# Preparing K and Q of an attention unit two units ahead, and starting a gated block one step earlier

## The chip, the cores and the metric

One core of a Trainium2 chip runs the whole program. The metric is the device time of one execution in microseconds (us), and less is better. The times given are medians of repeated executions; the profile is one execution more, with a time of its own.

## The reference

Attention over 4 batches, 8 heads, 576 positions, head size 64, with a threshold: scores lower than the row's maximum by more than tau are dropped. Then a gated feed-forward block on 2304 tokens of width 512, then a second one with a leaky ReLU:

```
scores = scale * q @ k^T                       # (4, 8, 576, 576)
keep   = scores >= max(scores) - tau
attn   = softmax(where(keep, scores, -1e9)) @ v
x      = attn as (2304, 512)
x      = (((x @ w1) * (x @ w2)) @ w3) @ w_out  # d_ff 1024
h      = x @ w_in                              # d_ff 2048
out    = maximum(0.01 * h, h) @ w_out2
```

All of it is fp32. The kernel multiplies `w3` by `w_out` once, so that the gated block is two products and one product more.

## The kernel before

The tokens are cut into six column groups of 384 (`gid` 0 to 5). Attention is cut into 32 units: a unit is a pair of heads `p` and a piece of one batch's queries that lies in one column group. A unit is made of steps, 80 in all. Units 0 to 3 (group 0), 12 to 19 (groups 2 and 3) and 28 to 31 (group 5) have three steps of 128 queries for each of the two heads. Units 4 to 11 (group 1) and 20 to 27 (group 4) have two steps, and are called tailed: the first (`c is None`) takes 64 queries of both heads as one block of 128 rows, the second takes 128 queries of each head. For the first, the two heads' Q blocks are put on the diagonal of a zeroed 128 x 128 tile, `qz`, or, where the operands are split, `qzs`. There is one of each.

Units 0 to 7 multiply fp32 operands in one pass. From unit 8 on (`PER = 8`) K and Q are split into a high part `qkh` and a low part `qkl` (fp32r), and a score takes three passes (`PASSES`). Before either, Q is multiplied by the scale `scl` on VectorE.

A step `n` of the main loop does this, in the order in which the code writes it:

- `load_halves` decodes a part of the weights (in the first steps), and `mask(n)` applies the threshold and normalises `e`: VectorE, with one multiplication on ScalarE (L298).
- `scale_unit(u + 1)` in the last step of a unit below 7: VectorE scales Q and writes `qz` (L213, L218).
- `scores(n + 1)`: TensorE (L267), row maximum on VectorE (L274), exponential on ScalarE (L275).
- `split_unit(u + 1)` in the first step of a unit: scale on VectorE (L231), `qkh` on ScalarE (L234), `qkl` on VectorE (L235), and for a tailed unit four copies into `qzs` on VectorE (L241).
- `weighted(u - 1)`, the product with V (L354), in the first step of a unit; its result goes to `xr` (L358).
- `transposes(n)`: a two-head step transposes `e` of head 0 into the PSUM tile `tp`, which ScalarE copies to `HH` (L338), then `e` of head 1 into the same tile, which VectorE copies (L334), then `tq`. There is one `tp`: the second four transposes wait for the first copy.
- Around the transposes stand pieces of six matmuls of a gated block (`gated`, `psab` L435 and `psh` L455). These are the filler. A two-head step has four of them, a tail step two.
- `load_v(u + 1)` and `load_unit(u + 2)` in the first step of a unit.

When the last unit of a column group is done, its gated block is put in a queue as due two steps later: `queue.append((n + 2, gid))`. At that step `split_x` splits the group's `xr` tiles (cast on ScalarE L366, difference on VectorE L367), and the block's pieces become the filler of the steps after. In the first steps there is no gated block; the product of `w3` and `w_out` (L405) and dummy matmuls stand between the transposes.

What sets the order: TensorE runs in the order of the code, by hand, from end to end. The queue of SP, which issues the loads, runs in the order of the code until the block of group 1 is due. VectorE, ScalarE and GpSimd are ordered during attention by a scheduler that simulates the program; a few instructions, the scaling among them, are kept in program order. From the second feed-forward block on all engines are ordered by hand.

Of the kernel before, what the change touches and what calls it, by code (L numbers as in the profile page):

```python
# [13 lines left out]
ALU = mybir.AluOpType  # L14
# [4 lines left out]
B, H, S, D = 4, 8, 576, 64  # L19
# [8 lines left out]
KS = D + S  # L28
# [7 lines left out]
UNITS = tuple(  # L36
    (b + i, p, g) for b in range(0, B, 2)
    for several in (((0, 0),), ((0, 1), (1, 0)), ((1, 1),)) for p in range(4) for i, g in several)
STEPS = tuple((u, c) for u, (b, p, g) in enumerate(UNITS) for c in PARTS[b % 2][g][2])
NS = len(STEPS)  # L40
PER = 8
# [7 lines left out]
def attention_gated_ffn(ctx: ExitStack, tc: tile.TileContext, qkv, tau, w3t, wout, w12, w2, out):  # L49
# [6 lines left out]
    nc = tc.nc  # L56

    def f(ap):
        return ap.bitcast(F32)
# [17 lines left out]
    qz = apool.tile([P, P], F32, name="qz")  # L77
# [4 lines left out]
    qzs = apool.tile([P, 2, P], F32R, name="qzs")  # L82
# [3 lines left out]
    scl = cpool.tile([P, 1], F32, name="scl")  # L86
# [77 lines left out]
    qk_t, vv_t = {}, {}  # L164

    def piece_of(u):

        b, p, g = UNITS[u]
        gq, gw, blocks = PARTS[b % 2][g]
        at = b * S + gq  # L170
        return gq, gw, blocks[0] is None, at // GW, at % GW
# [29 lines left out]
            nc.sync.dma_start(out=vv[:, a, :NK - 1], in_=src[:, :NK - 1])  # L201
            nc.sync.dma_start(out=vv[r, a, NK - 1], in_=src[r, NK - 1])

    def scale_unit(u):

        if u >= PER:
            return
        _, gw, tailed, _, _ = piece_of(u)
        qk = qk_t[u]
        if tailed:  # L210
            for a in range(2):
                o = a * D
                tc.keep_in_program_order(nc.vector.tensor_scalar(  # L213
                    out=qz[o:o + D, o:o + D], in0=qk[o:o + D, KS:KS + D], scalar1=scl[o:o + D],
                    scalar2=None, op0=ALU.mult))
        q = qk[:, KS + (D if tailed else 0):KS + gw]
        tc.keep_in_program_order(
            nc.vector.tensor_scalar(out=q, in0=q, scalar1=scl, scalar2=None, op0=ALU.mult))  # L218

    qks_t = {}  # L220

    def split_unit(u):

        if not PER <= u < len(UNITS):
            return
        _, gw, tailed, _, _ = piece_of(u)
        n = KS + gw
        qk = qk_t[u]
        q = qk[:, KS:n]
        tc.keep_in_program_order(  # L230
            nc.vector.tensor_scalar(out=q, in0=q, scalar1=scl, scalar2=None, op0=ALU.mult))  # L231
        hi = wld.tile([P, 1024], F32R, tag="st", name="qkh", bufs=4)
        lo = wld.tile([P, 1024], F32R, tag="st", name="qkl", bufs=4)
        nc.scalar.copy(hi[:, :n], qk[:, :n])  # L234
        nc.vector.tensor_tensor(out=lo[:, :n], in0=qk[:, :n], in1=f(hi[:, :n]), op=ALU.subtract)  # L235
        qks_t[u] = (hi, lo)
        if tailed:
            for i, part in enumerate((hi, lo)):
                for a in range(2):
                    r = slice(a * D, a * D + D)  # L240
                    nc.vector.tensor_copy(qzs[r, i, r], part[r, KS:KS + D])  # L241


    sc_t, e_t = {}, {}

# [36 lines left out]
    def mask(n):  # L282
        u, c = STEPS[n]
        sc, ths, st = sc_t.pop(n)
        for a, th in enumerate(ths):
            ev = e_t[n][:, a * S:a * S + S].rearrange("p (a b) -> p a b", a=2)
            nc.vector.scalar_tensor_tensor(  # L287
                out=ev, in0=sc[a][:, :, :HS], scalar=th, in1=ev, op0=ALU.is_ge, op1=ALU.mult,
                accum_out=st[:, a:a + 1])
        m = len(ths)  # L290
        nc.vector.tensor_scalar(out=st[:, :m], in0=st[:, :m], scalar1=1e-9, scalar2=None, op0=ALU.add)
        nc.vector.reciprocal(st[:, :m], st[:, :m])  # L292
        for a in range(m):
            ev = e_t[n][:, a * S:a * S + S]
            if a == m - 1:
                nc.vector.tensor_scalar(out=ev, in0=ev, scalar1=st[:, a:a + 1], scalar2=None, op0=ALU.mult)
            else:
                nc.scalar.activation(ev, ev, AF.Copy, scale=st[:, a:a + 1])  # L298
        if c is None:
            nc.gpsimd.tensor_copy(e_t[n][:, S:S + D], e_t[n][:, S - D:S])  # L300
# [42 lines left out]
    def weighted(u):  # L343

        _, gw, _, gid, at = piece_of(u)
        p = UNITS[u][1]
        vv = vv_t[u]
        HH, tail = he_t.pop(u), tl
        av = ps_w.tile([P, 512], F32, tag="w", name="av")
        for i in range(NK):  # L350
            for a in (1, 0):
                kc = (4, 0, 1, 2, 3)[i]
                rhs = (HH[:, kc, a] if kc < 4 else tail)[:, :gw]
                nc.tensor.matmul(  # L354
                    av[a * D:a * D + D, :gw], vv[:, a, kc], rhs, start=(i == 0), stop=(i == NK - 1))
        if (gid, p) not in x_t:
            x_t[gid, p] = xpool.tile([P, GW], F32, tag="xr", name="xr")
        nc.scalar.copy(x_t[gid, p][:, at:at + gw], av[:, :gw])  # L358
# [120 lines left out]
    load_v(0)  # L479
    load_unit(1)  # L480
    issue()
    scale_unit(0)
    halves_in = [0]
    folded = [0]

    def load_halves(k):
        for _ in range(k):
            if next(loads, 0) != 0:
                halves_in[0] += 1
# [9 lines left out]
    def fold_some(most, halves):  # L499

        while most and folded[0] < 2 * KF and piece(folded[0]) <= halves:
            next(folding, 0)
            folded[0] += 1
            most -= 1

    def keep_busy(k):

        scratch = ps_w.tile([P, 512], F32, tag="w", name="scratch")
        for _ in range(k):
            nc.tensor.matmul(scratch[:, :P], ident, ident, start=True, stop=True)  # L510
# [7 lines left out]
    queue = []  # L518
# [3 lines left out]
    def more(k):  # L522

        for _ in range(k):
            open_[0] = next(filler, False)

    for n in range(NS):
        u, c = STEPS[n]
        gid = piece_of(u)[3]
        weight = 1 if c is None else 2  # L530
        first_of_unit = n == 0 or STEPS[n - 1][0] != u
        last_of_unit = n == NS - 1 or STEPS[n + 1][0] != u
        decoded = halves_in[0]
        kh = 2 if n == 0 else 3
        load_halves(kh // 2)
        mask(n)
        if last_of_unit:
            scale_unit(u + 1)
        if n + 1 < NS:
            scores(n + 1)  # L540
        if n and first_of_unit:
            split_unit(u + 1)
        due += rate * weight

        if weigh:
            while open_[0]:
                more(1)
                due -= 1
            weighted(weigh.pop())
        k = max(0, int(due))  # L550
        due -= k
        parts = [(k + 2) // 3, (k + 1) // 3, k // 3]

        def fill(i):
            more(parts[i])
            if i < 2:
                fold_some(1, decoded)

        fill(0)
        pieces = transposes(n)  # L560
        next(pieces)
        fill(1)
        for _ in pieces:
            pass
        if last_of_unit:
            weigh.append(u)
        fill(2)
        if n < 3:
            keep_busy(7)
        if first_of_unit:  # L570
            load_v(u + 1)
            load_unit(u + 2)
        load_halves(kh - kh // 2)
        if last_of_unit and (n == NS - 1 or piece_of(u + 1)[3] != gid):
            queue.append((n + 2, gid))
        if queue and queue[0][0] == n:
            _, gid = queue.pop(0)
            while halves_in[0] < 32:
                load_halves(1)
            fold_some(2 * KF, 32)  # L580
            next(folding, 0)
            for _ in filler:
                pass
            if gid == 0:
                s_ld.close()
                gpool = s_ffn.enter_context(tc.tile_pool(name="gpool", bufs=8, reuse_waits="tile"))
                fpool = s_ffn.enter_context(tc.tile_pool(name="fpool", bufs=2, reuse_waits="tile"))
            if gid == 1:
                while halves_in[0] < 40:
                    load_halves(1)  # L590
                in_order.close()
            filler = gated(gid, split_x(gid))
            rate, due, open_[0] = 2.04, 0.0, False
# [38 lines left out]
    def issue():  # L632
        while len(raws) < min(used[0] + 3, len(order)):
            j, c = order[len(raws)]
            st = wld.tile([P, 1024], I32, tag="st", name="st", bufs=4)
            nc.sync.dma_start(out=st, in_=w2[j, :, c * 512:c * 512 + 512].bitcast(I32))
            raws.append(st)
# [305 lines left out]
    for n in range(total):  # L943
        ci, q = divmod(n, NQ)
# [71 lines left out]
```

## Time and profile before

| | before |
|---|---|
| median of 3 executions | 1050.05 us (1049.09 to 1051.96) |
| profiled execution | 1044.59 us |
| its span in the profile | 1042.8 us |
| TensorE matmul busy | 1006.2 us (96%) |
| VectorE / ScalarE / GpSimd busy | 644.2 / 574.5 / 235.3 us |
| granted TensorE clock, mean | 0.992 |
| TensorE idle in the span | 36.6 us |

The span starts with the first instruction on record and ends with the last. The 1.8 us by which the profiled execution's time exceeds it lie outside. Attention takes about the first 600 us of the span; the second feed-forward block has the rest.

### The profile page before, as it was taken

The page shows a single profiled execution, that of the slowest core. Times are in us where ns is not written, and L with a number is a line of the kernel's source. Part 1 is how long each engine was busy: PE and PEld are TensorE (multiplying, and loading weights), DVE is VectorE, ACT ScalarE, POOL GpSimd, SP SyncE. Part 2 cuts the span into 40 slices and gives each one's busy share as a digit, 9 for nine tenths or more (in the row PEclk, how much of TensorE's full clock was granted, in tenths as well). Part 3 has the DMA queues.
Part 4 walks back from the last instruction along what each step waited for, and adds up shares of the span by engine and source line. Part 5 has one row for each costly group of instructions (what it writes and reads, how often), then busy time and mean ns, then how long its engine had stood idle before and what let it go on. Part 6 is the DMA issues. An engine that isn't in the chain of part 4 may idle for free. (4 is left out here: it accounts for less than half of the span.)

```text
span 1042.8 us, 16142 instructions
## 1 busy us (share of the span) xinstructions
PE 1006.2 (96%) x5896; PEld 851.5 (82%) x5896; DVE 644.2 (62%) x1367; ACT 574.5 (55%) x1068; POOL 235.3 (23%) x219
## 2 busy tenths in 40 slices
PE   7899979999999999999999999999999999999998
PEld 5444458888888888888888899999988999999997
DVE  7889787788786777688877646275774111621111
ACT  5677674556565555455556536487874333543332
POOL 2335451100110110011001135245452111411110
PEclk9999989999999999999999999999999999999999
DMA  9644332223211111222211025578644953055401
GB/s 289 216 163 143 118 106 56 56 80 100 53 32 52 36 29 48 69 60 70 75 32 53 28 84 184 207 272 325 198 157 159 417 195 127 1 221 208 187 1 60
DMA packets 52126, 129.50 MB, mean 124 GB/s; under 512 B 15696, under 2 KB 30032, under 8 KB 48208
## 3 DMA queue, kind: packets, MB, share of 16 engines
q1 hardware_dynamic: 51904, 128.48, 35.9%
q8 instruction: 46, 0.75, 0.3%
q14 instruction: 32, 0.26, 0.1%
q10 hardware_dynamic: 144, 0.00, 0.0%
HBM read 95.95 MB, written 32.51 MB: 123 GB/s over the span
## 5 line engine op out<-in xcount | busy, mean ns | idle before, releaser
L435 PE MATMUL psab<-x,w 128*128 128x384 f32 x1152 | 233.6, 346 | 0.0
L925 PE MATMUL po<-dn,gg 128*128 128x512 f32 x864 | 222.9, 390 | 0.0
L435 PEld LDWEIGHTS psab<-x,w 128*128 128x128 f32 x1152 | 195.7, 188 | 11.4 <-DVE e L287 5.4
L925 PEld LDWEIGHTS po<-dn,gg 128*128 128x128 f32 x864 | 160.0, 188 | 22.0
L890 PE MATMUL ps<-h,uph 128*128 128x384 f32 x672 | 172.8, 338 | 1.1 <-DVE sum L872 0.6
L872 DVE TENSOR_TENSOR sum<-snap,ps 128x384 f32<-128x384 f32 x72 | 39.8, 552 | 173.9 <-PE ps L890 162.4
L275 ACT ACTIVATE e<-sc,nm 128x576 f32<-128x576 f32 x144 | 100.9, 738 | 70.8 <-DVE nm L274 70.7
L890 PEld LDWEIGHTS ps<-h,uph 128*128 128x128 f32 x672 | 123.5, 188 | 15.1 <-DVE sum L872 1.3
L448 POOL TENSOR_TENSOR gt<-at,gt 128x384 fp32r<-128x384 f32 x48 | 50.2, 1045 | 376.3 <-ACT gt L447 376.3
L274 DVE TENSOR_REDUCE nm<-sc 128x1 f32<-128x576 f32 x144 | 103.6, 752 | 40.8 <-PE sc L267 40.0
L287 DVE SCALAR_TENSOR_TENSOR e<-sc,nm,e 128x576 f32<-128x576 f32 x144 | 113.1, 815 | 13.5 <-ACT e L275 8.7
L455 PE MATMUL psh<-gt,w 128*128 128x384 f32 x576 | 114.1, 344 | 0.0
L890 PE MATMUL ps<-h,upl 128*128 128x384 f32 x336 | 113.1, 337 | 0.0
L880 POOL TENSOR_TENSOR gg<-sum,gg 128x384 fp32r<-128x384 f32 x48 | 50.4, 1050 | 254.3 <-ACT gg L879 230.5
L455 PEld LDWEIGHTS psh<-gt,w 128*128 128x128 f32 x576 | 98.1, 188 | 4.8 <-issue 2.4
L332 PE MATMUL tp<-ident,e 128*128 128x128 f32 x512 | 78.5, 276 | 10.9 <-ACT HH L338 10.7
L332 PEld LDWEIGHTS tp<-ident,e 128*128 128x128 f32 x512 | 63.5, 141 | 26.9 <-ACT HH L338 13.0
L867 ACT COPY snap<-ps 128x384 f32<-128x384 f32 x72 | 34.3, 477 | 88.7 <-PE ps L890 88.7
L298 ACT ACTIVATE e<-e,nm 128x576 f32<-128x576 f32 x64 | 49.7, 777 | 40.8 <-DVE nm L292 40.3
L334 DVE COPY HH<-tp 128x512 f32<-128x512 f32 x64 | 44.2, 690 | 39.5 <-PE tp L332 39.4
L354 PE MATMUL av<-HH,vv 128*64 128x384 f32 (+1 forms) x512 | 67.6, 406 | 0.0
L877 ACT ACTIVATE sum<-sum 128x384 f32<-128x384 f32 x72 | 37.8, 525 | 48.1 <-DVE sum L872 48.1
(117 smaller groups left out, 1428.6 us busy)
## 6 DMA issues: line engine op xcount, KB each, us to landing
st<-in_w SPq DMA_DIRECT2D x48, 512.0 KB, 5.6
dn<-dn_d SPq DMA_DIRECT2D x10, 1024.0 KB, 7.4
uph<-up_d SPq DMA_DIRECT2D x10, 896.0 KB, 8.4
upl<-up_d SPq DMA_DIRECT2D x10, 896.0 KB, 4.6
vv<-in_qkv SPq DMA_DIRECT2D x64, 128.0 KB, 2.2
raw<-in_w3t SPq DMA_DIRECT2D x8, 1024.0 KB, 6.7
dn_d<-dn SPq DMA_DIRECT2D x8, 1024.0 KB, 6.7
up_d<-uph SPq DMA_DIRECT2D x8, 896.0 KB, 4.6
```

What stands on the lines that cost most here:

```text
L274: nc.vector.tensor_reduce(out=nm, in_=sc[a][:, :, :HS], op=ALU.max, axis=AX.XY, negate=True)
L275: nc.scalar.activation(e[:, a * S:a * S + S].rearrange("p (a b) -> p a b", a=2), sc[a][:, :, :HS], AF.Exp, bias=nm)
L287: nc.vector.scalar_tensor_tensor(out=ev, in0=sc[a][:, :, :HS], scalar=th, in1=ev, op0=ALU.is_ge, op1=ALU.mult, accum_out=st[:, a:a + 1])
L298: nc.scalar.activation(ev, ev, AF.Copy, scale=st[:, a:a + 1])
L332: nc.tensor.transpose(tp[:, kc], e[:, k0:k0 + P], ident)
L354: nc.tensor.matmul(av[a * D:a * D + D, :gw], vv[:, a, kc], rhs, start=(i == 0), stop=(i == NK - 1))
L435: nc.tensor.matmul(ps, w12_t[i][:, a, mat * 512 + kk * P:mat * 512 + kk * P + P], xt[kk][:, c], start=(m == 0), stop=(m == 11))
L448: nc.gpsimd.tensor_tensor(out=gt[i][:, 1], in0=at, in1=f(gt[i][:, 0]), op=ALU.subtract)
L455: nc.tensor.matmul(ps, w34_t[i // 2][:, a, i % 2, o * P:o * P + P], gt[i][:, c], start=(m == 0), stop=(m == 23))
L880: eng.tensor_tensor(out=gg[:, 1], in0=gf, in1=f(gg[:, 0]), op=ALU.subtract)
L890: nc.tensor.matmul(ps, (uph, upl)[a][:, wi, i * P:i * P + P], hs[k][:, c, i], start=(opens[k] and m == 0), stop=(m == 5), skip_group_check ...
L925: nc.tensor.matmul(po_t[o], gg[:, c, t * P:t * P + P], dn[:, i, a], start=(q == 0 and seen[o] == 1 and m == 0), stop=(q == NQ - 1 and seen ...
```

## The change

The code that scales Q and the code that splits K and Q become one function, `prepare_unit`, which runs for unit `u + 2` in the last step of unit `u`, behind `scores(n + 1)` (before: the scaling for `u + 1` in the last step of `u`, ahead of `scores(n + 1)`; the splitting for `u + 1` in the first step of `u`). For the first eight units it scales the whole piece, the tail block too. The copies that place the tail block, `place_tail(u + 1)`, run in the first step of unit `u`, behind `mask(n)` and ahead of `scores(n + 1)`, one step before the tail's scores. A gated block is due one step behind its last unit's last step, not two.

```diff
-    def scale_unit(u):
-        if u >= PER:
-            return
...
-        if tailed:
-            for a in range(2):
-                o = a * D
-                tc.keep_in_program_order(nc.vector.tensor_scalar(
-                    out=qz[o:o + D, o:o + D], in0=qk[o:o + D, KS:KS + D], scalar1=scl[o:o + D],
-                    scalar2=None, op0=ALU.mult))
-        q = qk[:, KS + (D if tailed else 0):KS + gw]
...
-    def split_unit(u):
-        if not PER <= u < len(UNITS):
+    def prepare_unit(u):
+        if u >= len(UNITS):
             return
         _, gw, tailed, _, _ = piece_of(u)
         n = KS + gw
...
         q = qk[:, KS:n]
         tc.keep_in_program_order(
             nc.vector.tensor_scalar(out=q, in0=q, scalar1=scl, scalar2=None, op0=ALU.mult))
+        if u < PER:
+            return
         hi = wld.tile([P, 1024], F32R, tag="st", name="qkh", bufs=4)
         lo = wld.tile([P, 1024], F32R, tag="st", name="qkl", bufs=4)
         nc.scalar.copy(hi[:, :n], qk[:, :n])
         nc.vector.tensor_tensor(out=lo[:, :n], in0=qk[:, :n], in1=f(hi[:, :n]), op=ALU.subtract)
         qks_t[u] = (hi, lo)
-        if tailed:
...
+    def place_tail(u):
+        if u >= len(UNITS) or not piece_of(u)[2]:
+            return
+        if u < PER:
+            for a in range(2):
+                r = slice(a * D, a * D + D)
+                tc.keep_in_program_order(nc.vector.tensor_copy(qz[r, r], qk_t[u][r, KS:KS + D]))
+            return
+        for i, part in enumerate(qks_t[u]):
+            for a in range(2):
+                r = slice(a * D, a * D + D)
+                nc.vector.tensor_copy(qzs[r, i, r], part[r, KS:KS + D])
...
-    scale_unit(0)
+    prepare_unit(0)
...
         mask(n)
-        if last_of_unit:
-            scale_unit(u + 1)
+        if first_of_unit:
+            place_tail(u + 1)
         if n + 1 < NS:
             scores(n + 1)
-        if n and first_of_unit:
-            split_unit(u + 1)
+        if n == 0:
+            prepare_unit(1)
+        if last_of_unit:
+            prepare_unit(u + 2)
...
-            queue.append((n + 2, gid))
+            queue.append((n + 1, gid))
```

The lines of the changed kernel's loop stand six lower than before's (L267 is L261 there). Three places show what moves.

**TensorE, steps 13 and 14**, where the gated block of group 0 begins. `sc` are scores, `tp` and `tq` transposes, `psab` the block's first product. Before:

```order
L267 MATMUL sc<-qk,qz 128x288 x2
L332 MATMUL tp<-ident,e 128x128 x8
L335 MATMUL tq<-ident,e 128x128
L267 MATMUL sc<-qk 128x288 x4
L354 MATMUL av<-tl,vv_89 64x192 x2
L354 MATMUL av<-HH,vv_89 64x192 x8
L435 MATMUL psab<-x,w_577 128x384 x6
```

And now:

```order
L261 MATMUL sc<-qk,qz 128x288 x2
L429 MATMUL psab<-x,w_578 128x384 x12
L326 MATMUL tp<-ident,e 128x128 x4
L429 MATMUL psab<-x,w_578 128x384 x6
L326 MATMUL tp<-ident,e 128x128 x4
L329 MATMUL tq<-ident,e 128x128
L429 MATMUL psab<-x,w_578 128x384 x6
L261 MATMUL sc<-qk 128x288 x4
```

The block's first 24 matmuls stand around the transposes of step 13, where nothing stood between them before.

**ScalarE, the last step of a three-step unit of group 2**, from the exponentials (`e<-sc,nm`) on. `at` and `gt` belong to the gated block, `HH<-tp` is the copy that frees `tp`. Before:

```order
L275 ACTIVATE e<-sc,nm 128x576 x2
L443 COPY at<-psab 128x384
L338 COPY HH<-tp 128x4x128
L298 ACTIVATE e<-e,nm 128x576
L336 COPY tl<-tq 128x128
L447 CAST gt<-at 128x384
```

And now:

```order
L269 ACTIVATE e<-sc,nm 128x576 x2
L437 COPY at<-psab 128x384
L220 CAST qkh<-qk 128x1024
L332 COPY HH<-tp 128x4x128
L330 COPY tl<-tq 128x128
L292 ACTIVATE e<-e,nm 128x576
L441 CAST gt<-at 128x384
```

The cast that makes `qkh`, which stood in the step behind, now stands ahead of the copy that frees `tp`. It stands so in the last step of 14 units; the other steps have it behind the copy.

**VectorE, a tailed unit of group 4.** Before, in the unit's second step:

```order
L274 TENSOR_REDUCE nm<-sc 128x1 x2
L278 TENSOR_SCALAR nm<-nm,cb 128x2
L231 TENSOR_SCALAR qk<-qk,scl 128x192
L287 SCALAR_TENSOR_TENSOR e,nm<-sc,nm,e 128x576 x2
L235 TENSOR_TENSOR qkl<-qk,qkh 128x832
L241 COPY qzs<-qkh 64x64 x2
L291 TENSOR_SCALAR nm<-nm 128x2
L324 COPY tl<-tq 64x64 x2
L241 COPY qzs<-qkl 64x64 x2
L292 RECIPROCAL nm<-nm 128x2
```

And now, in the step ahead of that:

```order
L215 TENSOR_SCALAR qk<-qk,scl 128x192
L281 SCALAR_TENSOR_TENSOR e,nm<-sc,nm,e 128x576
L439 TENSOR_TENSOR at<-psab,at 128x384
L221 TENSOR_TENSOR qkl<-qk,qkh 128x832
L236 COPY qzs<-qkh 64x64
L285 TENSOR_SCALAR nm<-nm 128x1
L236 COPY qzs<-qkh 64x64
L328 COPY HH<-tp 128x4x128
L236 COPY qzs<-qkl 64x64 x2
L286 RECIPROCAL nm<-nm 128x1
L290 TENSOR_SCALAR e<-e,nm 128x576
L268 TENSOR_REDUCE nm<-sc 128x1 x2
```

The four copies into `qzs`, which were the last work ahead of the next tail's scores, stand a step earlier, ahead of the two-head maxima (`TENSOR_REDUCE x2`), together with the difference `qkl` of the unit behind.

## Rows read from the trace of the kernel before

**Rows 1.** The page, part 1: busy time, share of the span, instructions of each engine.

```profile
PE 1006.2 (96%) x5896; PEld 851.5 (82%) x5896; DVE 644.2 (62%) x1367; ACT 574.5 (55%) x1068; POOL 235.3 (23%) x219
```

**Rows 2.** Busy time by stretch: stretch, length, engines, clock, DMA share, GB/s.

```profile
100.00:150.00 50.00, 40.99 (x168) 22.61 (x166) 40.60 (x86) 36.21 (x66) 25.77 (x21) 0.86 0.40 120
...
135.00:140.00 5.00, 3.11 (x8) 2.06 (x8) 3.79 (x8) 4.18 (x9) 3.17 (x3) 0.50 0.72 216
```

**Rows 3.** The waits of TensorE: us in total, times, longest.

```profile
PE tp L332 <- ACT HH L338: 10.7, 8, 2.9
PE sc L267 <- DVE qzs L241: 7.2, 20, 1.3
PE sc L267 <- DVE qk L218: 3.5, 2, 2.6
PE sc L267 <- PE psab L435: 0.7, 1, 0.7
```

**Rows 4.** TensorE's timeline: start, us, operation [idle before <- releaser].

```profile
43.93 0.66 PE L332 MATMUL tp<-ident,e 128*128 128x128 f32 x4 [2.94 <-ACT HH L338]
...
136.18 2.26 PE L267 MATMUL sc<-qk,qz 128*128 128x288 f32 x4 [4.07 <-issue]
...
140.54 1.11 PE L332 MATMUL tp<-ident,e 128*128 128x128 f32 x4 [1.25 <-ACT HH L338]
...
150.72 1.21 PE L267 MATMUL sc<-qk,qz 128*128 128x288 f32 x4 [1.54 <-issue]
```

**Rows 5.** VectorE's timeline, steps 13 and 14.

```profile
135.55 0.53 DVE L213 TENSOR_SCALAR qz<-qk,scl 64x64 f32<-64x64 f32 x2
...
139.15 1.08 DVE L367 TENSOR_TENSOR x<-xr,x 128x384 fp32r<-128x384 f32 x1
```

**Rows 6.** Timelines of TensorE and VectorE in group 4; durations of L235 (min/median/max ns).

```profile
497.54 0.53 PE L267 MATMUL sc<-qkh,qzs 128*128 128x288 f32 x2 [1.31 <-DVE qzs L241]
504.56 1.42 DVE L274 TENSOR_REDUCE nm<-sc 128x1 f32<-128x576 f32 x2 [1.45 <-PE sc L267]
L235 DVE TENSOR_TENSOR qkl<-qk,qkh x24: 1017/1122/1226, 174.5 to 562.5; 128x832 fp32r<-128x832 f32 x12, 128x1024 fp32r<-128x1024 f32 x12
```

**Rows 7.** TensorE's timeline: a two-head step with filler, and one without.

```profile
575.18 2.35 PE L435 MATMUL psab<-x,w 128*128 128x384 f32 x12
577.38 0.60 PE L332 MATMUL tp<-ident,e 128*128 128x128 f32 x4
577.73 1.31 PE L435 MATMUL psab<-x,w 128*128 128x384 f32 x6
578.88 0.60 PE L332 MATMUL tp<-ident,e 128*128 128x128 f32 x4
...
246.56 0.66 PE L332 MATMUL tp<-ident,e 128*128 128x128 f32 x4 [0.68 <-ACT HH L338]
```

**Rows 8.** ScalarE's timeline in the same steps; durations of L234 (min/median/max ns).

```profile
577.63 0.48 ACT L443 COPY at<-psab 128x384 f32<-128x384 f32 x1
578.01 0.59 ACT L338 COPY HH<-tp 128x512 f32<-128x512 f32 x1
245.92 0.58 ACT L338 COPY HH<-tp 128x512 f32<-128x512 f32 x1
L234 ACT CAST qkh<-qk x24: 882/976/1070, 173.4 to 561.2; 128x832 fp32r<-128x832 f32 x12, 128x1024 fp32r<-128x1024 f32 x12
```

**Rows 9.** Timelines of TensorE and GpSimd at the start.

```profile
27.16 1.31 PE L267 MATMUL sc<-qk 64*128 64x288 f32 x8 [2.58 <-DVE qk L218]
26.91 1.31 POOL L152 TENSOR_TENSOR w<-t,lw 128x512 int32<-128x512 int32 x1 [0.80 <-ACT t L146]
```

**Rows 10.** Loads of K and Q: SP's timeline; issues of 148 to 151 and of 4 to 20 us.

```profile
149.64 0.59 SPq L185 DMA_DIRECT2D qk<-in_qkv  x1
qk<-in_qkv SPq DMA_DIRECT2D x2, 192.0 KB, 3.1
qk<-in_qkv SPq DMA_DIRECT2D x4, 240.0 KB, 6.1
```

More of the change, by code (lines that the diff above doesn't have):

```diff
@@ L202, in load_v @@
             nc.sync.dma_start(out=vv[r, a, NK - 1], in_=src[r, NK - 1])
-    def scale_unit(u):
-        if u >= PER:
-            return
-        _, gw, tailed, _, _ = piece_of(u)
-        qk = qk_t[u]
-        if tailed:
-            for a in range(2):
-                o = a * D
-                tc.keep_in_program_order(nc.vector.tensor_scalar(
-                    out=qz[o:o + D, o:o + D], in0=qk[o:o + D, KS:KS + D], scalar1=scl[o:o + D],
-                    scalar2=None, op0=ALU.mult))
-        q = qk[:, KS + (D if tailed else 0):KS + gw]
-        tc.keep_in_program_order(
-            nc.vector.tensor_scalar(out=q, in0=q, scalar1=scl, scalar2=None, op0=ALU.mult))
     qks_t = {}
-    def split_unit(u):
-        if not PER <= u < len(UNITS):
+    def prepare_unit(u):
+        if u >= len(UNITS):
             return
@@ L236, in split_unit @@
         qks_t[u] = (hi, lo)
-        if tailed:
[L238 to L241, printed above, removed]
+    def place_tail(u):
[10 more added lines that the diff above has]
+                nc.vector.tensor_copy(qzs[r, i, r], part[r, KS:KS + D])
     sc_t, e_t = {}, {}
```

## The prediction

> **What bounds the kernel now.** I read the page's busy times first: TensorE is busy for 1006.2 us [rows 1], so of the span of 1042.8 us 36.6 us are idle, and no edit here takes a matmul away. What can be won is idle time, and time at the lower clock. The table by stretches shows where: the worst one behind the start is 100 to 150 us, with 41.0 us busy at a mean granted clock of 0.86, and in it 135 to 140 us ran at 0.50, the lower of TensorE's two levels, 1.2 GHz [rows 2]. The list of TensorE's waits then names what can go: 10.7 us for the copy that frees `tp`, 7.2 us for the `qzs` copies, 3.5 us for a scale, 0.7 us of another kind [rows 3]. The timelines show each in its place. The profiled execution took 1044.59 us, 5.46 us less than the median of the runs, 1050.05. I make the sum on the profiled execution and carry the difference to the median.
>
> A measurement of this kernel can tell some 0.3% from no change, so 3.15 us: "faster" is below 1046.9, "slower" above 1053.2.
>
> **A: group 0's block one step earlier.** At steps 13 and 14 TensorE waits 4.07 us before the tail's scores and 1.25 us between the transposes, and works at half rate: four scores matmuls take 2.26 us there and 1.21 us at 150.72 [rows 4]. The first wait ends when VectorE, busy with weights, has reached the scale that writes `qz` at 135.55 [rows 5]. The change puts that copy a step earlier, and 24 filler matmuls into the step. At full rate 24 take 2.20 us for twelve (575.18 to 577.38) and 1.15 for each six (577.73 to 578.88), so 4.5 us [rows 7]. They lie in 5.3 us of idle time and leave a later stretch by 4.5 us. The 1.54 us at 150.72 wait for the same kind of `qz` scale [rows 4], and the 0.7 us at 163.65, put down to `psab` [rows 3], are I think a third; both go. Sum +6.7 us. The bounds: the block can begin only when the `x` differences are there, and the one in this stretch stands at 139.15 [rows 5], 3 us behind the scores; if they hold TensorE, and it stays at half rate, the 24 cost 4.5 us more and A is +2.2. At the other end the half-rate stretch goes as well, +8.
>
> For the other groups the same edit moves filler from one step to the neighbour. The steps without filler at groups 1 to 2 and 4 to 5 are still one each; what stands in them now is the product with V, and the second four transposes wait 0.68 us at such a place [rows 7]. I give each 0.35 us more for a copy that can come ahead of `HH`'s: −0.7 us, between 0 and −1.
>
> **B: tail copies a step earlier.** All 20 `qzs` waits, 7.2 us [rows 3], are of the form at 497.54, where the copies are VectorE's last work ahead of the scores [rows 6]. A step earlier, they have six microseconds and more to spare: +7.2 us. What they delay is the two-head maximum behind them. It stands behind one `qkl` of 1.02 us more and four copies; VectorE was idle for 1.45 us before it, waiting for TensorE [rows 6]. What is over is some 0.3 us, and the maxima feed `e`, which is due a step later: nothing. If that cover is gone, 0.3 us for ten units is 3 us, so B lies between 4 and 7.2.
>
> **C: the start.** The scale at which TensorE waited 2.58 us is now two units ahead. But the fold behind those scores needs a weight that GpSimd ends at 26.91 + 1.31 = 28.2, where TensorE reached it at 28.4 [rows 9]. So 2.58 is the upper bound, 0 the lower, and I take 0.6, near the lower: 0.2 us at the fold and some of the chain of maxima behind.
>
> **D: the cast that makes `qkh`.** This speaks against the change. In the last step of a unit the ScalarE queue now has the cast ahead of the copy that frees `tp`. Before, `at` ended at 578.11, the copy took 0.58 us, and six filler matmuls between the two transposes hid it: they end at 578.88 [rows 7, 8]. Now: 578.11, a cast of 1.07 us to 579.18, the copy to 579.76. At 246 TensorE started 0.06 us behind such a copy's end (245.92 + 0.58 = 246.50, then 246.56) [rows 7, 8], so 579.82: 0.94 us late. By the order this holds in seven last steps: 6.6 us. Three more have the cast ahead, with `at`, `ht` or nothing around it, which makes 0.35, 0.83 and 0.85 us by the same walk; four tailed units have a cast of 0.88 us [rows 8], and 0.46 us each, 1.84 us. Sum −10.4 us. The bounds: the ends overlap by some 0.1 us in the rows, and the cast need not stand idle for VectorE, so −8; if each of the 14 waits the whole 0.94 it is −13.
>
> The Trainium skill, "Perfetto Trace Analysis", section Per-instruction lifecycle, says that ScalarE's and VectorE's queues are strictly first in, first out, and that TensorE can take only weight loads ahead. By that rule a cast ahead of the copy costs its whole time wherever the filler is short, and the term is near the −10.4 that the rows make; without it the term would be near 0. The trace agrees in that the copy at 577.63 to 578.01 follows `at` directly, though its transposes were over before.
>
> **E: loads.** In the hand-ordered part of SP's queue, units 6 to 11, the scale stands in VectorE's queue in program order, and K and Q of that unit have just been issued: 149.64 us, landing 3.1 us after, 152.7 [rows 10], 3.6 us behind the tail's scores if these come 1.54 us sooner [rows 4]. By the rows of a tail's chain on VectorE the scale is reached some 3.9 us behind the scores. Nothing, then; this is rival 4.
>
> **The sum.** +6.7 − 0.7 + 7.2 + 0.6 − 10.4 = +3.4 us. The profiled execution goes from 1044.59 to about 1041.2; the median from 1050.05 to **1046.6**.
>
> **The rivals.**
>
> 1. *ScalarE's casts don't hold TensorE* (D is 0): 6.7 − 0.7 + 7.2 + 0.6 = 13.8 us less, 1036.2. For it: the filler hides copies of this size today, and the list has only 8 waits for `HH` in 64 copies. Against: the order, and 0.27 us of slack (578.88 less 578.60) against a cast of 0.88 us or more [rows 7, 8].
>
> 2. *The first block yields little.* TensorE's clock fell to 0.50 behind the wait of 4.07 us, and did not behind one of 2.94 us at 43.93, where transposes ran at 0.66 us [rows 4]. If VectorE is still late for scores or `x` in step 13, the idle time is in another place, the stretch is at half rate, and A is 2.2: the sum is −1.1 us, 1051.2. For it: VectorE was busy for 40.6 of these 50 us [rows 2], and `x` is needed earlier now. Against: a scale and a `qz` write leave just that place. The Trainium skill, "TensorE: Matmul & The Clock Gate", section What's actually happening, has half rate as the default and activity as what releases it; by that rule filler in step 13 also keeps the clock up, and A would lie above my 6.7.
>
> 3. *Slower: a late load holds VectorE.* One mechanism: units 6 to 11, whose scale is now issued two units ahead, right behind the loads. VectorE's queue stops at the scale until K and Q have landed; the `HH` copy of head 1, `at` of the gated block and the next maxima stand behind it. Loads at the start took 6.1 us to land, not 3.1 [rows 10]. With 5.5 us it would be 2.4 us later than in E, less the slack of 0.3 and some 0.7 that the next scores leave: 1.4 to 1.5 us for six units, 9 us. The sum is then −5.6 us: 1055.7. It decides from 0.7 us for each unit beyond the slack on. For it: the scale is kept in program order, so the scheduler can't put it back. Against: the loads of 148 us land in 3.1, and traffic is less there than at the start.
>
> 4. *The change doesn't do what it says*: tail copies in the scheduler's order are late for another reason (there is one `qzs`, and it is free only when the tail's scores before have read it), and B is 0. The sum is −3.8 us: 1053.8.
>
> **How the numbers follow.** My forecast, with its bounds on A, B and D, reaches from 1041.5 to 1050.5: chance 0.45, of which 0.33 lies below 1046.9. Rival 1 has 0.13, all faster. Rival 2 has 0.20, all within 0.3%. Rival 3 has 0.14, all slower. Rival 4 has 0.08, half within 0.3% and half slower. So faster 0.46, within 0.3% 0.12 + 0.20 + 0.04 = 0.36, slower 0.18. The range reaches from rival 1's time to just above rival 4's: 1036 to 1054.5, and leaves out most of rival 3 and the lower part of rival 1.
>
> **What the profile after would show.** Right: no `qzs` waits of any size in TensorE's list; 14 or so more waits for `HH`, of 0.4 to 1 us, at the last steps of units, 10 us and more beyond the 10.7; 100 to 150 us busier by 4 us or more, at a clock above 0.86; `psab` ahead of step 13's transposes; GpSimd in place of the scale as what TensorE waits for at the fold near 28 us. Wrong: `HH` waits as before (rival 1); a stretch at 0.50 still, or waits for `x` near 137 us (rival 2); VectorE idle for a load ahead of L215 between 140 and 220 us (rival 3); tail scores that still wait for `qzs` (rival 4).

## The result: 1038.7 us, 11 us less than before

The changed kernel takes 1038.74 us (median of 6 executions, 1036.44 to 1040.41), the kernel before, run beside it, 1049.80. The ratio is 0.9893, with an interval of 0.9875 to 0.9911, so some 11.2 us less. Forecast were 1046.6 us, or 3.4 us less: the sign and the range held, the size did not.

The profile of the changed kernel has a span of 1038.5 us, only 4.3 us less than the one read ahead of the prediction. That pair misleads: before's profile was 5.5 us below its median, the new one 1.7 us above. The mean granted clock goes with it. Before, run again, had spans of 1043.0 to 1050.2 us at mean clocks of 0.985 to 0.992 (47 executions, mean 0.9886); the changed kernel 1032.5 to 1038.5 us at 0.990 to 0.998 (10 executions, mean 0.993). At the same 0.992, spans are 1043.0 and 1043.5 before, 1036.0 to 1036.9 after: some 6.8 us. By this estimate, from two and three executions, the rest, some 4 us, goes with the changed kernel's higher mean clock; no run separates the two.

TensorE's waits after, the first lines of the list (us in total, times, longest):

```profile
PE tp L326 <- ACT HH L332: 12.9, 17, 2.9
PE ps L399 <- POOL w L152: 4.6, 2, 2.5
PE psab L429 <- DVE x L361: 2.6, 1, 2.6
```

Against [rows 3]: `qzs` is gone as a releaser, there are 17 waits for `HH` where there were 8, and one wait for an `x` difference is new. The sum of `HH` waits grew by 2.2 us only, where the prediction looked for 10 and more: eleven waits behind 240 us are new and come to 5.5 us, and two of 1.9 and 1.25 us ahead of 150 us are no longer waits for `HH`.

The stretches that answer to [rows 2]:

```profile
100.00:150.00 50.00, 43.33 (x175) 25.09 (x173) 40.73 (x80) 36.39 (x67) 28.40 (x24) 0.90 0.35 114
...
135.00:140.00 5.00, 3.24 (x14) 2.48 (x14) 4.89 (x14) 5.00 (x10) 2.80 (x3) 1.00 0.72 232
140.00:145.00 5.00, 3.11 (x11) 3.02 (x12) 4.93 (x9) 3.44 (x8) 4.17 (x3) 0.63 0.31 86
145.00:150.00 5.00, 5.00 (x28) 4.13 (x28) 3.17 (x8) 2.73 (x6) 3.77 (x4) 0.69 0.00 0
```

TensorE is busy for 2.3 us more in these 50 us, where the prediction looked for 4 or more. The half-rate stretch begins later but is still there. Its place on TensorE's timeline, the answer to [rows 4]:

```profile
135.70 1.21 PE L261 MATMUL sc<-qk,qz 128*128 128x288 f32 x4 [0.93 <-PE tq L314]
136.53 1.97 PE L429 MATMUL psab<-x,w 128*128 128x384 f32 x9
138.86 0.44 PE L429 MATMUL psab<-x,w 128*128 128x384 f32 x1 [0.36 <-ACT x L360]
141.89 1.01 PE L429 MATMUL psab<-x,w 128*128 128x384 f32 x2 [2.58 <-DVE x L361]
142.69 1.05 PE L326 MATMUL tp<-ident,e 128*128 128x128 f32 x4
143.40 2.27 PE L429 MATMUL psab<-x,w 128*128 128x384 f32 x6
```

The wait of 4.07 us ahead of the scores is now 0.93. Filler takes its place at full rate, until the last of its four `x` tiles is missing: VectorE makes that difference at 140.20:

```profile
140.20 1.63 DVE L361 TENSOR_TENSOR x<-xr,x 128x384 fp32r<-128x384 f32 x1
```

Behind the 2.58 us TensorE works at the lower level (six `psab` in 2.27 us, 1.31 in [rows 7]). That is the mechanism of rival 2.

The casts that term D spoke of: TensorE, then ScalarE, in the last step of a three-step unit (the answer to [rows 7, 8]).

```profile
271.53 0.60 PE L326 MATMUL tp<-ident,e 128*128 128x128 f32 x4
271.88 1.32 PE L429 MATMUL psab<-x,w 128*128 128x384 f32 x6
273.75 0.65 PE L326 MATMUL tp<-ident,e 128*128 128x128 f32 x4 [0.55 <-ACT HH L332]
```

```profile
271.78 0.48 ACT L437 COPY at<-psab 128x384 f32<-128x384 f32 x1
272.16 1.05 ACT L220 CAST qkh<-qk 128x1024 fp32r<-128x1024 f32 x1
273.11 0.59 ACT L332 COPY HH<-tp 128x512 f32<-128x512 f32 x1
```

The order is as forecast, and the cast does hold TensorE. But the second four transposes start 2.22 us behind the first four (271.53 to 273.75), against 1.50 before [rows 7]: 0.72 us, not 0.94. The three ScalarE instructions overlap by 0.1 us each.

Tail scores of two neighbouring units, after and then before:

```profile
434.14 0.30 PE L261 MATMUL sc<-qkh,qzs 128*128 128x288 f32 x1
434.27 0.30 PE L261 MATMUL sc<-qkl,qzs 128*128 128x288 f32 x1
...
445.74 0.30 PE L261 MATMUL sc<-qkh,qzs 128*128 128x288 f32 x1
```

```profile
445.09 0.37 PE L267 MATMUL sc<-qkh,qzs 128*128 128x288 f32 x1 [0.17 <-DVE qzs L241]
...
445.97 0.53 PE L267 MATMUL sc<-qkh,qzs 128*128 128x288 f32 x2 [0.38 <-DVE qzs L241]
...
457.75 0.37 PE L267 MATMUL sc<-qkh,qzs 128*128 128x288 f32 x1 [0.16 <-DVE qzs L241]
```

The period is 12.66 us before and 11.60 after, 1.06 us less, although the two waits recorded in such a unit make only 0.55 us. Idle time is counted from a matmul's modelled end, and that lies behind the time at which the next one starts when nothing holds it: after, where no wait stands between them, these matmuls start every 0.13 us and are drawn 0.30 long.

### The profile page after: what moved, and what is told of

Read it like the earlier page. It is cut to its first block, busy times and chain, and to the rows that moved or that the text cites. A ratio compares the mean times of both kernels' runs of the same rounds, so it can differ in the third digit from the quotient of the medians.

```text
span 1038.5 us, 16135 instructions
## 1 busy us (share of the span) xinstructions
PE 1006.0 (97%) x5896; PEld 852.3 (82%) x5896; DVE 646.2 (62%) x1367; ACT 572.4 (55%) x1068; POOL 238.9 (23%) x219
## 5 line engine op out<-in xcount | busy, mean ns | idle before, releaser
L281 DVE SCALAR_TENSOR_TENSOR e<-sc,nm,e 128x576 f32<-128x576 f32 x144 | 113.1, 815 | 10.4 <-ACT e L269 4.7
L399 PE MATMUL ps<-wo,w 128*128 128x512 f32 x128 | 60.3, 615 | 4.6 <-POOL w L152 4.6
```

Of the source, the lines that this page charges most:

```text
L281: nc.vector.scalar_tensor_tensor(out=ev, in0=sc[a][:, :, :HS], scalar=th, in1=ev, op0=ALU.is_ge, op1=ALU.mult, accum_out=st[:, a:a + 1])
L399: nc.tensor.matmul(ps, w3_t[i][:, j * P:j * P + P], wo_t[j // 2][:, (j % 2) * 512:(j % 2) * 512 + 512], start=(j == 0), stop=(j == KF - 1))
```

## The experiments

The times beside a run are medians; the kernel before is that of the same set of runs (1048.63, 1049.22 and 1048.73 us for the first four, the next four and the last two).

**The kernel before once more** (no edit).

> The kernel before once more, with a profile of each execution. The two profiles differ by 4.2 us, the medians by 11.1 us. Theory: the profile of before was an early end of its spread, and the missing 7 us are idle time or time at the lower clock in the first 150 us, which changes between executions; then spans lie at 1046 to 1050 and the profile shows a lower mean clock than 0.992 or more idle time ahead of 150 us, and nothing new behind it. Rival: the 7 us lie in the stages behind (150 us on), so that waits there are longer than in the profile that was read.

Measured: 1047.74 us, ratio 0.9992 (0.9979 to 1.0004). Span of the profile 1045.7 us. From the product with V of unit 3 (av, at 130.72 us here, 127.97 in the first profile) to the end of the attention both profiles agree within 0.1 us in every stage; the 2.8 us lie ahead of that, at the lower clock. The half-rate stretch around step 13 is there in both:

```profile
135.00:140.00 5.00, 1.07 (x2) 0.84 (x3) 4.86 (x15) 4.92 (x10) 2.80 (x3) 0.74 0.70 222
140.00:145.00 5.00, 3.75 (x14) 2.61 (x14) 3.29 (x9) 4.03 (x8) 3.76 (x3) 0.50 0.29 84
145.00:150.00 5.00, 5.00 (x34) 3.38 (x33) 4.86 (x10) 4.35 (x9) 3.28 (x4) 0.73 0.00 0
```

So the theory holds for these two profiles: the start differs, nothing behind it, and this makes 2.8 of the missing 7 us. The ten executions have spans of 1044.9 to 1047.4 us, somewhat below the 1046 to 1050 that were expected. This profile, not the first, is the one to set stages against.

**The block's due step alone.**

```diff
-            queue.append((n + 2, gid))
+            queue.append((n + 1, gid))
```

> Before, with the gated block due one step behind its last unit and nothing else. If the moved filler alone fills the idle time of steps 13 and 14 (term A of the prediction), 5 to 7 us less than before, and 24 psab matmuls stand around step 13's transposes. If what made room was the earlier qz copy (the scale that VectorE reached at 135.55 us), TensorE still waits some 4 us ahead of the tail's scores and the gain is 3 us or less. The 20 qzs waits of 7.2 us stay in either case.

Measured: 1044.52 us, ratio 0.9959 (0.9941 to 0.9977), 4.1 us less. TensorE still waits for `qz`:

```profile
137.30 2.26 PE L267 MATMUL sc<-qk,qz 128*128 128x288 f32 x4 [4.07 <-issue]
...
154.94 1.21 PE L267 MATMUL sc<-qk,qz 128*128 128x288 f32 x4 [2.76 <-issue]
```

The filler stands in step 13, but the idle time ahead of it is whole, and the 1.54 us of the next unit [rows 4] grew to 2.76. What the edit did gain lies elsewhere: the two long `qzs` waits of 1.31 us (one is in [rows 6]) are gone, since `x` is no longer split between the tail copies; 16 waits of 4.3 us are left of the 20 of 7.2 that were expected to stay. VectorE before, ahead of the wait at 497.54:

```profile
495.19 0.39 DVE L241 CAST qzs<-qkh 64x64 fp32r<-64x64 f32 x2
...
496.15 1.03 DVE L367 TENSOR_TENSOR x<-xr,x 128x384 fp32r<-128x384 f32 x2
497.10 0.39 DVE L241 CAST qzs<-qkl 64x64 fp32r<-64x64 f32 x2
```

The tailed groups are 1.3 and 1.2 us shorter. That I had counted in B. The filler that moved gains little alone: the stage from unit 3's product with V to unit 7's grows from 55.83 to 58.97 us, and the stretch behind the last product with V shrinks from 441.1 to 437.1.

**The preparation alone.**

```diff
-            queue.append((n + 1, gid))
+            queue.append((n + 2, gid))
```

(against the changed kernel.)

> The changed kernel with the gated block due two steps behind, as before. Left are the preparation two units ahead and the early tail copies: the qzs waits go (7.2 us), the waits for HH behind the cast stay as in the changed kernel's profile (some 5.5 us at 11 places of 0.5), and the qz waits of 1.5 and 0.7 us go. So 3 to 5 us less than before and 5 to 7 us more than the changed kernel. If the early preparation is what the medians' 11 us come from, it is within 3 us of the changed kernel.

Measured: 1047.88 us, ratio 0.9989 (0.9975 to 1.0003): nothing that can be told from before, though every `qzs` wait is gone. The casts take it back: against the profile of before once more, the tailed units 8 to 11 and 20 to 27 take 3.4 and 3.2 us less (from one product with V to another, here and below), the three-step units 12 to 19 and 28 to 31 take 4.5 and 1.5 us more. With no filler in step 13 the idle time has only moved from the scores to the transposes:

```profile
136.50 1.21 PE L261 MATMUL sc<-qk,qz 128*128 128x288 f32 x4 [0.93 <-PE tq L314]
140.35 1.11 PE L326 MATMUL tp<-ident,e 128*128 128x128 f32 x4 [2.64 <-ACT e L292]
143.08 1.12 PE L326 MATMUL tp<-ident,e 128*128 128x128 f32 x4 [1.62 <-ACT HH L332]
```

The 3 to 5 us that were expected did not come. The two halves give 4.1 and 0.75 us alone and 11 together.

**The cast behind the copy.**

```diff
-        if last_of_unit:
-            prepare_unit(u + 2)
...
         next(pieces)
+        if last_of_unit:
+            prepare_unit(u + 2)
```

and `tc.keep_in_program_order` around the `qkh` cast and the `HH` copy from step 13 on.

> The changed kernel with the preparation written behind the first four transposes, and the qkh cast and the copy that frees tp kept in program order on ScalarE, so that the copy comes first. If the cast ahead of the copy costs what the changed kernel's profile shows (11 waits of about 0.5 us, 5.5 us), 5 to 6 us less than the changed kernel and no HH waits of 0.5 us behind 260 us. If another instruction takes the cast's place as what is late (qkl and the tail copies on VectorE now start later), the HH waits go and qzs or e waits come, and the time is within 2 us of the changed kernel's.

Measured: 1033.45 us, ratio 0.9853 (0.9827 to 0.9878), 0.4% under the changed kernel's ratio, some 4.2 us. In groups 2 and 3, where the changed kernel needs 179.5 us for eight units and before 175.3, it is 175.75: D is gone there. In tailed units another instruction took the cast's place in every second one, as the rival had it:

```profile
435.34 0.51 ACT L443 CAST gt<-at 128x384 fp32r<-128x384 f32 x1 [1.36 <-DVE at L441]
435.76 0.58 ACT L332 COPY HH<-tp 128x512 f32<-128x512 f32 x1
```

The copy is kept in program order and so stands behind a `gt` cast that waits for VectorE; TensorE pays for it:

```profile
436.39 0.66 PE L326 MATMUL tp<-ident,e 128*128 128x128 f32 x4 [0.46 <-ACT HH L332]
```

With such waits the stages from unit 3's product with V to unit 11's take 106.1 us, where the two profiles of the changed kernel take 104.1 and 103.1. So by the stages the casts alone cost more than these 4.2 us.

**The split of the last `x` earlier.**

```diff
         nc.scalar.copy(x_t[gid, p][:, at:at + gw], av[:, :gw])
+        if u <= 3:
+            split_one(gid, p)
```

where `split_one` is the body of `split_x`'s loop, and the tail step's `HH` copy of step 12 is kept in program order.

> The changed kernel with the split of each xr tile of group 0 written right behind its product with V, and the tail step's HH copy kept behind the last cast, so that the last x cast stands one ScalarE instruction after xr (before it four) and the x difference ahead of two weight instructions on VectorE. If group 0's first block is held by a late x and by the lower clock that follows (rival 2 of the prediction), the waits of 0.36 and 2.58 us ahead of psab shrink by 1 us or more, the mean clock of the executions rises above the changed kernel's 0.9925, and the time falls by 1 to 4 us. If what bounds the step is the chain from the maxima over e to the transposes, the idle time comes back as a wait for e or HH and the time is the changed kernel's within 1 us.

Measured: 1037.24 us, ratio 0.9881 (0.9861 to 0.9900). The wait for the `x` difference falls from 2.58 to 1.09 us and that for the cast goes, a wait of 1.30 us for `HH` comes, and the stage from the product with V of unit 3 to that of unit 7 takes 52.90 us, where the changed kernel's two profiles (the second is below) take 54.85 and 53.78.

```profile
138.82 0.62 PE L439 MATMUL psab<-x,w 128*128 128x384 f32 x2 [1.09 <-DVE x L364]
142.24 0.66 PE L328 MATMUL tp<-ident,e 128*128 128x128 f32 x4 [1.30 <-ACT HH L334]
```

The clock is 1.00 from 130 to 155 us in this profile and was not in those two, so the 0.9 to 1.95 us hold what the clock gave, too. By the times it is 1.5 us against the changed kernel, which the intervals can't tell from nothing: inconclusive by time, and in its stage not told apart from the clock. By the waits both readings had a part: an `x` that is late, and behind it the chain over `e` and `HH`.

**Both, as the best version.** The early `x`, and the cast kept behind the copy in the last steps of three-step units and of units 22 and 24:

```diff
+    def behind(n):
+        u = STEPS[n][0]
+        last = n == NS - 1 or STEPS[n + 1][0] != u
+        return last and (u in (22, 24) if piece_of(u)[2] else u >= 12)
...
-        if last_of_unit:
+        if last_of_unit and not behind(n):
             prepare_unit(u + 2)
...
         next(pieces)
+        if behind(n):
+            prepare_unit(u + 2, True)
```

(the second argument keeps the cast in program order.)

> The early x and, in the last steps of three-step units and of two tailed units, the qkh cast kept behind the copy that frees tp (where gt or nothing stands between, the cast is left). Removing each cast that held TensorE should give 5 to 7 us, as the run with all casts behind did, and the early x what it gives alone: 1029 to 1033 us. If the two don't add up (the clock is at its level already in most executions), 1033 to 1034 us.

Measured: 1030.20 us (1029.99 to 1030.86), ratio 0.9821 (0.9805 to 0.9838). It beats both kernels: 19 us under before. Against the run above, which differs by the casts alone, the ratio falls by 0.0060: D is 6.3 us. Groups 2 and 3 take 175.7 us here and 179.5 in the run above. Its waits:

```profile
PE tp L335 <- ACT HH L341: 9.5, 9, 2.9
PE ps L418 <- POOL w L152: 4.6, 2, 2.5
...
PE psab L448 <- DVE x L373: 1.1, 1, 1.1
```

**The tail copies late again, with the early split.**

```diff
-        if first_of_unit:
+        if last_of_unit:
             place_tail(u + 1)
```

> The changed kernel with the tail copies written in a unit's last step, ahead of the tail's scores, as before; the preparation stays two units ahead. If it is the early splitting that removed the qzs waits, the scheduler takes the qzs copies ahead (they wait for nothing then), the tailed units keep their period of 11.6 us, and only the qz copies of units 5 to 7, which are kept in program order, are late again: 2 to 4 us more than the changed kernel. If it is the place of the copies, the period of the tailed units is 12.65 us again and the kernel is about 10 us slower than the changed one.

Measured: 1041.57 us, ratio 0.9930 (0.9914 to 0.9946), some 3.9 us more than the changed kernel by the ratios. The tailed groups are the changed kernel's within 0.1 us; what is back is the wait for `qz`:

```profile
138.50 1.78 PE L261 MATMUL sc<-qk,qz 128*128 128x288 f32 x3 [3.92 <-issue]
```

So the `qzs` waits went because the split is early, not because the copies are written early; the scheduler puts those early by itself, here too a step ahead of the tail's scores. For `qz`, whose copies are kept in program order, the place decides.

**Early scale, split as before.**

```diff
-        if first_of_unit:
+        if first_of_unit and u + 1 < PER:
             place_tail(u + 1)
...
-        if last_of_unit:
+        if last_of_unit and u + 2 < PER:
             prepare_unit(u + 2)
+        if first_of_unit and u + 1 >= PER:
+            prepare_unit(u + 1)
+            place_tail(u + 1)
```

> The changed kernel with the units from 8 on split as before (one unit ahead, in the first step, copies behind the difference); the scale and the qz copies of units below 8 stay early and the block is due one step behind. This leaves the prediction's term A without B and D. If filler and early qz copies need each other (each alone gave little: 4.1 us for the block's due step, 0.75 us for the preparation), the stretch from the product with V of unit 3 to that of unit 7 is the changed kernel's (54.9 us), the mean clock is its 0.9925, and the time is 7 to 9 us under before's. If the gain of the two together comes from the split units instead, it is the time of the block's due step alone, 4 us under before's.

Measured: 1039.76 us, ratio 0.9912 (0.9895 to 0.9928), so 9.2 us less than before by term A, the early scale at the start, and the two long `qzs` waits, which are gone here as with the due step alone. The stage from unit 3's product with V to unit 7's is 54.63 us. In this profile the clock stayed up, behind the same wait for `x` (2.56 us):

```profile
135.00:140.00 5.00, 2.03 (x11) 1.46 (x10) 4.90 (x9) 4.74 (x9) 3.34 (x3) 1.00 0.75 209
140.00:145.00 5.00, 5.00 (x35) 4.18 (x37) 4.90 (x11) 3.47 (x7) 4.04 (x4) 1.00 0.12 36
```

And still the stage is no shorter than the 54.85 and 53.78 us of the changed kernel, whose clock fell in it.

**The tails alone.** The kernel with the cast behind the copy, with the block due at `n + 2`.

> All casts behind the copy that frees tp, preparation two units ahead, tail copies early, and the block due two steps behind as before: the prediction's term B without A and D. The stages of the profiles so far give 9 us less in the tailed units of groups 1 and 4 (10 units of 1.05 us less each, from periods of 12.65 and 11.6 us) and nothing else, less what group 0's block leaves idle in steps 13 and 14 as before: 1040 to 1043 us. If the recorded idle time is the whole cost of a qzs wait, 7.2 us less at most and with the wait for e and HH at 140 us some 1045 us.

Measured: 1042.12 us, ratio 0.9934 (0.9918 to 0.9951): 6.9 us less. Units 8 to 11 take 2.5 us less than before and units 20 to 27 take 5.1 less, in which the waits of 0.46 us behind `gt` are included: 7.6 us, where 9 were expected. The stage from unit 3's product with V to unit 7's is 2.0 us longer. With this, the parts add up within the intervals: 9.2 (the run above) + 6.9 = 16.1, where the kernel with both and without D has 15.4 by its ratio; less D of 5.8 (the preparation alone has 0.9989, this one 0.9934) it is 10.3, where the changed kernel has 11.2. The 16.1 counts the two long `qzs` waits twice: no `qzs` wait is left here, with the block due two steps behind, and they are gone in the run above, with the split as before.

**The changed kernel once more.**

> The changed kernel once more, beside the run above. Its first profile was the slowest of six executions, with the clock at 0.63 to 0.69 from 140 to 150 us. If the half-rate stretch in group 0's first block is there in some executions only, this one's mean clocks spread from 0.990 to 0.995 again, and an execution with the higher clock is 3 us shorter or more; the waits for HH behind 230 us are the same ten or eleven of about 0.55 us in any.

Measured: 1037.71 us, ratio 0.9890 (0.9870 to 0.9910). Its four executions have mean clocks of 0.991, 0.992, 0.995 and 0.998, and times of 1038.88, 1038.07, 1037.36 and 1034.38 us. The profile has the wait for `x` with 2.57 us, a shorter half-rate stretch (0.66 from 140 to 145 us, then 1.00), and behind 230 us the same `HH` waits as the first within 0.02 us. That is as expected, but for the spread: the clocks reach 0.998, and of the two executions above 0.992 one is 3.7 us shorter or more and one 0.7.

## Why the prediction was right in its sign and short in its size

By its own terms (gains positive, by the ratios above):

| term | forecast | measured | from |
|---|---|---|---|
| A, with the other groups' −0.7 | +6.0 | +9.2 | early scale and due step without early split |
| B | +7.2 | +6.9, beside A +6.2 | the tails alone; 15.4 − 9.2 |
| C | +0.6 | none found | the start, below |
| D | −10.4 | −4.2 to −6.3 | three pairs that differ by the casts |
| sum | +3.4 | +11.2 | the changed kernel |

**The range held in part by luck.** The measured 1038.74 us lies below the better end that I gave my own forecast, 1041.5, in the part of the range that only rival 1 reached, and rival 1 did not come true. Nor do that forecast's ends follow from the bounds: with A, B and D all at their better ends the sum is 7.1 us, 1043.0, and at their worse ends −6.9 us, 1056.9.

**A was right in its mechanism, and its 9.2 us hold a part that I had in B.** The filler went where it was forecast, and it needed the early `qz` copy: with the due step alone the wait of 4.07 us stayed, with the preparation alone it moved to the transposes. The stage from unit 3's product with V to unit 7's shows it: 55.83 us before, 58.97 with the due step alone, 56.33 with the preparation alone, 54.85 and 53.78 with both, though with the due step 24 more matmuls stand in it. Of the 3.2 us beyond the forecast, 2.5 are the two long `qzs` waits, which the due step removes by itself. The 0.7 left is within the run's interval of 1.7 us either way.

I had written the clock into A's bounds ("the half-rate stretch goes as well, +8") and not into the sum. In the runs that stretch is whole in both profiles of before (for ten us and more between 135 and 150 us, 0.50 where it fills a slice), shorter in both of the changed kernel and absent in that of the early scale, and the mean clock of the executions rises from 0.9886 to 0.993. What time this gave in the block is not shown: the stage took 54.63 us with the clock up and 53.78 with it down for a part. The rule of the Trainium skill that I had set beside rival 2, "TensorE: Matmul & The Clock Gate", section What's actually happening (half rate is the default and activity releases it), agrees with the rise of the mean clock; that A came out above 6.7 us for this reason is not shown.

**B: the sum was about right, for a wrong reason.** The recorded idle time of 0.55 us for a unit understates what a unit pays, 1.06 us by the period; the waits behind `gt` took a part of that back. And not all 20 waits are of the form at 497.54, as I had it: that row and one more are the two waits of 1.31 us, with `x` differences between the copies. They were not B's alone, as the due step removes them, and so does the preparation. Without them I had 4.6 us, and beside A the runs give some 6.2.

**C was nothing.** From the start to the product with V of unit 3 the profiles take 127.97, 130.72 and 129.09 us with the scale as before, and 128.61 to 131.43 in the nine profiles with the early scale. The scale's wait of 2.58 us turned into one of 2.50 us for GpSimd's weight, as the prediction had said it could:

```profile
30.29 3.70 PE L399 MATMUL ps<-wo,w 128*128 128x512 f32 x8 [2.50 <-POOL w L152]
```

**D was the step that failed.** The mechanism is shown: the cast stands ahead of the copy, TensorE waits, and taking the cast behind gives the time back. The strict order of ScalarE's queue, the rule cited there ("Perfetto Trace Analysis" of the Trainium skill, section Per-instruction lifecycle), agrees with the rows of the changed kernel: the transposes end at 272.13, and the copy starts at 273.11, behind the cast. The row that I had named for it, the copy at 578.01, does not show it: its transposes end only 0.03 us before (577.38 + 0.60).

The size was wrong twice: 10.4 us were forecast, and the three pairs give 4.2 (all casts behind, with new waits in their place), 5.8 and 6.3. I laid the durations end to end, which gave 0.94 us; the rows overlap by 0.1 us at each of two joints, and it is 0.72. I had seen this overlap, and put it into a bound instead of into the walk. And I gave a price to 14 places by the order alone. In the trace the cast stands ahead of the copy in the last steps of 18 units (12 to 29), eleven waits follow, one of them of 0.16 us, and in the other seven TensorE has no wait. In a tailed unit, for one, the cast is over before the transposes are:

```profile
436.63 0.88 ACT L220 CAST qkh<-qk 128x832 fp32r<-128x832 f32 x1
437.66 0.59 ACT L332 COPY HH<-tp 128x512 f32<-128x512 f32 x1 [0.15 <-PE tp L326]
```

**The rivals.** Rival 1 (casts hold nothing) fell, though its time, 1036.2 us, is the nearest to the measured one. Rival 2 (the first block yields little) is half there: `x` is late by 2.58 us, but the mean clocks are 0.990 to 0.998, before 0.985 to 0.992, and A is 9.2 us, not 2.2. Rival 3 (a late load) is there in the rows and costs nothing: VectorE waits for K and Q at two places behind the start,

```profile
171.01 0.32 DVE L215 TENSOR_SCALAR qk<-qk,scl 128x192 f32<-128x192 f32 x1 [0.53 <-DMA qk<-in_qkv]
220.19 0.42 DVE L215 TENSOR_SCALAR qk<-qk,scl 128x384 f32<-128x384 f32 x1 [1.12 <-DMA qk<-in_qkv]
```

and TensorE has no wait between 163 and 237 us. Rival 4 (tail copies late anyway) fell.

**The base was off as well.** I made the sum on the fastest execution of before of all that were seen, and carried 5.46 us over unchanged. In the profile taken again 2.8 us, half of that gap, are the start at the lower clock; it was no constant to carry.

## What to carry to other kernels

Two edits can each be worth little because either alone only moves a wait: filler without its operand, or an operand without filler. Price them together, at the place where both meet. Price a wait by the period of the loop with and without it, not by the idle time in front of an instruction; and when an instruction goes into a full queue, walk with start-to-start distances of the same instructions in the trace, and look at which places the queue is full at all.

## What was not expected of the hardware

The granted clock behind like waits was not the same. Behind the wait of 2.6 us for `x` it was 0.63 and 0.69 in one profile of the changed kernel, 0.66 and then 1.00 in another, and 1.00 from 130 to 155 us with the early scale alone (2.56 us) and with all casts behind the copy (2.55 us). Whether what ran ahead of the wait, or chance, decides this is left open; no run varied that alone.
